# Attention and two MoE layers on one core: loads of sums moved ahead of raw weights, low parts on VectorE, norms and output copies on ScalarE

## The chip, the cores and the metric

One NeuronCore of a Trainium2 chip runs the whole computation. The metric is the device time of one execution in microseconds (us). Five engines with in-order queues take part: PE (TensorE, the matmuls; its weight loads are listed as PEld), DVE (VectorE), ACT (ScalarE), POOL (GpSimd) and SP (SyncE, which here only issues DMAs).

## The reference

Three steps follow one another; the output of each is the input of the next.

1. Attention over q, k, v of 4 batches, 8 heads, 576 tokens, 64 values. *Downsampled*: q, k, v are averaged over groups of 4 tokens to 144, a softmax attention runs on those, and its result is repeated 4 times. *Local*: a softmax attention over the keys with |i - j| < 4. The two results are added and laid out as x, 2304 tokens x 512.
2. MoE 1: `(silu(x @ w_gate) * (x @ w_val)) @ w_out`, inner width 1536.
3. MoE 2: `h = x @ w_in; (h * clip(h + 3, 0, 6) / 6) @ w_out`, inner width 2048.

## The kernel before

**Weights.** The weights arrive as raw 8-byte floats. The chip decodes each to fp32 once, in block 0: `decode_a` (L208, ScalarE, the top bits) and `decode_b` (L217, VectorE, the rest). The fp32 form is written to DRAM (`kept`) and loaded again in the later blocks. A *unit* is 128x512 weights. `split_unit` cuts it into a high part (L228, ScalarE, tile `wr`) and a low part, weight minus high part (L231, also `wr`). `POOL_SPLIT = {1: 4}` puts every fourth low part of block 1 on GpSimd (17 of 68); all others are VectorE's. `prefetch(i)` issues the steps of a unit ahead of its use: the raw load 8 units ahead, the load from `kept` 6, the decoding 5 and 4, the split 2.

**Blocks.** The tokens go through in five blocks of 512, 384, 512, 512 and 384 tokens (0 to 4). In each, 68 units follow one another in `run_unit`. Phase 1 (36 units) is MoE 1: G (`pG`), V (`pV`) and O (`aO`). Phase 2 (32 units) is MoE 2: H (`pH`) and P (`aP`). Each product is made of three matmul passes from high and low parts. Between the products VectorE and ScalarE work on the inner values: `sl` (L953, L959), `h` (L962, L963), `gV` and `gH` (L964, L965), and the high and low part of x in `put_cols` (L265, L266). At the end of a block `put_out` copies the four (or three) output banks, even ones by ScalarE (L1014), odd ones by VectorE (L1012), and SP sends them out.

**Attention inside the blocks.** x of the first batch is made in the front, before block 0 (`first_batch`: scores `fS`, row maxima `fnm`, exponentials `held`, values `fO`, sums `fxf`). The local attention of the other three batches is cut into chunks that run on VectorE beside the products of blocks 0 to 3: scores (L781, L784) in phase 1, values (L818 to L824, tile `o`) in phase 2; then PE turns `o` around (`px`, L838), `xf` adds the downsampled part (L847) and `put_cols` writes x of a later block. The downsampled attention of batch b+1 runs in block b, for b = 0, 1, 2:

- `down_sums`: twelve loads (`nq`, `nk`, `nv`, four each) and two GpSimd additions for each (L290, L291). For batch 1 they stand in the front, with six buffers; for batches 2 and 3 in phase 1 of blocks 1 and 2, with two buffers, driven once in two units.
- `down_main`, in phase 2: for each of four head pairs the scores (`pS`, L872), the maxima and exponentials (L697 on VectorE, L701 on ScalarE), then `norm_d` one unit later: L707 and L708 on VectorE make 1/sum (72x2), L709 on VectorE multiplies the 72x288 probabilities by it. Then PE transposes them (`pPT`, L715) and multiplies by the values (`pO`, L722).

**What sets the order.** The code issues instructions in the order above, and a scheduler makes one in-order queue for each engine. In the front, `behind` and `late` keep the steps of the weights and the loads in the order in which the code writes them. Buffers also order things: raw weights have four (`w64`), so the load of unit 4 waits on SP's queue for the decoding of unit 0.

Of the kernel before, what the change touches and what calls it, by code (L numbers as in the profile page):

```python
# [10 lines left out]
F32 = mybir.dt.float32  # L11
# [6 lines left out]
AF = mybir.ActivationFunctionType  # L18
# [15 lines left out]
CLOAD = (0, 4)  # L34

EARLY = 6

POOL_SPLIT = {1: 4}


@with_exitstack
def tile_kernel(
# [85 lines left out]
    def behind(ins):  # L128

        if front[0]:  # L130
            tc.keep_in_program_order(ins)
# [93 lines left out]
    def split_unit(i):  # L225
        s = view(w32[i // 2], i)
        r = sp.tile([P, 2, NC, P], F32R, tag="wr", name=f"wr{i}", bufs=4)
        behind(nc.scalar.activation(r[:, 0], s, AF.Copy))  # L228
        n = POOL_SPLIT.get(units[i][2])
        eng = nc.gpsimd if n and i % n == 0 else nc.vector  # L230
        behind(eng.tensor_tensor(r[:, 1], s, r[:, 0].bitcast(F32), op=ALU.subtract))  # L231
        split[i] = r

    def prefetch(i):
# [37 lines left out]
    def load_down(b, what, half, hh, alloc, eng):  # L272
        src = {"q": q, "k": k, "v": v}[what]
        t = alloc(f"n{what}{b}_{half}{hh}")
        late(
            eng, t,
            src[b, hh * 4:hh * 4 + 4, half * NJH * 4:(half + 1) * NJH * 4, :].rearrange("h (j t) d -> j h t d", t=4),
        )
        nat[b, what, half, hh] = t

    def down_sums(b, dn, qk, alloc, bufs, eng):
        keys = [(w, half, hh) for w in "qkv" for half in range(2) for hh in range(2)]
        for w in "qkv":
            dn[w] = sp.tile([NJH, 2, H, D], F32, tag="dn" + w, name=f"dn{w}{b}", bufs=1)
        for m in range(bufs):
            load_down(b, *keys[m], alloc, eng)
        for n, key in enumerate(keys):
            w, half, hh = key
            t = nat.pop((b, *key))
            nc.gpsimd.tensor_tensor(t[:, :, 0:2], t[:, :, 0:2], t[:, :, 2:4], op=ALU.add)  # L290
            nc.gpsimd.tensor_tensor(dn[w][:, half, hh * 4:hh * 4 + 4], t[:, :, 0], t[:, :, 1], op=ALU.add)  # L291
            if n + bufs < len(keys):
                load_down(b, *keys[n + bufs], alloc, eng)
            yield
# [23 lines left out]
    def first_batch():  # L318
# [6 lines left out]
        with tc.tile_pool(name="fp", bufs=1) as fp:  # L325
# [41 lines left out]
            def load_vd(n):  # L367
                hh, half = divmod(n, 2)
                t = fp.tile([NJH, H // 2, 4, D], F32, tag="vnat", name=f"vd4{half}{hh}", bufs=2)
                late(  # L370
                    nc.sync, t,
                    v[0, 4 * hh:4 * hh + 4, half * NJH * 4:(half + 1) * NJH * 4, :].rearrange(
                        "h (j t) d -> j h t d", t=4
                    ),
                )
                nc.gpsimd.tensor_tensor(t[:, :, 0:2], t[:, :, 0:2], t[:, :, 2:4], op=ALU.add)
                nc.gpsimd.tensor_tensor(vd[:, half, 4 * hh:4 * hh + 4], t[:, :, 0], t[:, :, 1], op=ALU.add)
# [20 lines left out]
            def values_of(i):  # L398
                return vw[i][:, i % 2].rearrange("p (h d) -> p h d", h=H)

            for n in range(2):
                load_vd(n)
                load_vw(n)
            prefetch(-LR)
            prefetch(1 - LR)
            for n in range(2, 4):
                load_vd(n)
                load_vw(n)
            load_vw(4)
            assert NT == 5  # L410
            prefetch(2 - LR)

            tmp = spare("tmp")
            at = 0
# [232 lines left out]
            for c in range(NC):  # L647
                load_T("q", c)
                load_T("k", c)
                if c:  # L650
                    down_scores(c - 1)
                sums(c)
                if c == 2:
                    prefetch(3 - LR)
                if c >= 2:
                    down_trans(c - 2)
            down_values(0)
            scores(0)
            down_scores(3)
            down_trans(2)  # L660
# [45 lines left out]
    def norm_d(pd, sd):  # L706
        nc.vector.tensor_scalar(sd, sd, EPS, 4.0, op0=ALU.add, op1=ALU.mult)  # L707
        nc.vector.reciprocal(sd, sd)  # L708
        nc.vector.tensor_tensor(pd, pd, sd[:, :, None].to_broadcast([NJH, 2, NJ]), op=ALU.mult)  # L709

    def trans_d(pd, ps):
        pt = ps[:NJH, :2 * NJ].rearrange("p (g j) -> p g j", g=2)
# [292 lines left out]
    def put_out(bi, e, ps):  # L1005
        if e == 0:

            done = sp.tile([P, NC, 2, UMAX * UT], F32R, tag="x2", name=f"os{bi}", bufs=1).bitcast(F32)
            state["os"] = done.rearrange("p c a t -> p (c a t)")
        os = state["os"][:, e * DM:(e + 1) * DM]  # L1010
        if e % 2:
            nc.vector.tensor_copy(os, ps)  # L1012
        else:
            nc.scalar.activation(os, ps, AF.Copy)  # L1014
        gu = starts[bi] + 2 * e
        (b, u), (b1, _) = divmod(gu, NG), divmod(gu + 1, NG)
        for n, m in ((0, 2),) if b == b1 else ((0, 1), (1, 1)):
            b, u = divmod(gu + n, NG)
            if b == 0:
                dst = out[(gu + n) * UT:(gu + n + m) * UT, :]  # L1020
            else:
                dst = flat(out, (b * S + u * 4) * DM, [[DM, 4 * m], [SL * DM, NSEG], [1, DM]])
            nc.sync.dma_start(dst, os[n * UT:(n + m) * UT, :])
# [115 lines left out]
```

## Time and profile before

| | us |
|---|---|
| median of 3 runs | 1001.62 (1001.51 to 1006.58) |
| the profiled execution | 1001.4 |
| its span | 999.3 |
| PE busy | 955.3 (96%) |
| DVE busy | 787.6 (79%) |
| ACT busy | 510.6 (51%) |
| POOL busy | 137.2 (14%) |

The profile is of one execution. Its own time is 2.1 us over its span (what lies around the span), and 0.2 us below the median. A busy share is a mean over stages that differ: in the front PE waits for attention, in phase 2 of block 1 VectorE has more to do than in blocks 3 and 4, and GpSimd has work in the front and in blocks 1 and 2 only. The mean granted TensorE clock of the span is 0.984 of full speed.

### The profile page before, as it was taken

The page shows a single profiled execution, that of the slowest core. Times are in us where ns is not written, and L with a number is a line of the kernel's source. Part 1 is how long each engine was busy: PE and PEld are TensorE (multiplying, and loading weights), DVE is VectorE, ACT ScalarE, POOL GpSimd, SP SyncE. Part 2 cuts the span into 40 slices and gives each one's busy share as a digit, 9 for nine tenths or more (in the row PEclk, how much of TensorE's full clock was granted, in tenths as well). Part 3 has the DMA queues.
Part 4 walks back from the last instruction along what each step waited for, and adds up shares of the span by engine and source line. Part 5 has one row for each costly group of instructions (what it writes and reads, how often), then busy time and mean ns, then how long its engine had stood idle before and what let it go on. Part 6 is the DMA issues. An engine that isn't in the chain of part 4 may idle for free.

```text
span 999.3 us, 13482 instructions
## 1 busy us (share of the span) xinstructions
PE 955.3 (96%) x4800; PEld 796.1 (80%) x4800; DVE 787.6 (79%) x1251; ACT 510.6 (51%) x1058; POOL 137.2 (14%) x130
## 2 busy tenths in 40 slices
PE   8769999999998999879999999999999999999997
PEld 5658888778797987767878777788888788999996
DVE  6698986899999879998985699999346995545653
ACT  4667566766543475444333654443335444544653
POOL 5680000000068211103630000000000000000000
PEclk9789999999999999999999999999999999999999
DMA  9979999377677532245753212354322233533331
GB/s 194 211 222 318 304 321 319 115 248 262 222 238 219 179 107 80 85 148 164 222 172 115 76 64 93 124 191 141 104 85 90 85 100 111 157 125 124 124 123 50
DMA packets 83655, 160.72 MB, mean 161 GB/s; under 512 B 19460, under 2 KB 51716, under 8 KB 83588
## 3 DMA queue, kind: packets, MB, share of 16 engines
q1 hardware_dynamic: 78692, 142.03, 45.4%
q10 hardware_dynamic: 4896, 17.83, 5.1%
q8 instruction: 38, 0.62, 0.3%
q14 instruction: 29, 0.24, 0.1%
HBM read 137.29 MB, written 22.54 MB: 160 GB/s over the span
## 4 chain that ended last, share of the span: by engine, by line
PE 78%; DVE 14%; ACT 2%; issue 2%; DMA 2%; SPq 0%; ACTq 0%; DVEq 0%
PE aP L989 19%; PE pH L947 19%; PE aO L989 13%; PE pG L947 12%; PE pV L947 11%; DVE wr L231 3%; DVE pr L781 2%; DVE sc L784 1%; PE pS L872 1%; DVE gV L965 1%; ACT held L561 1%; PE pO L722 1%; DMA w<-kept 1%; DVE sl L959 1%; DMA w<-in_moe_w_val_dram 1%
## 5 line engine op out<-in xcount | busy, mean ns | idle before, releaser
L231 DVE TENSOR_TENSOR wr<-w,wr 128x512 fp32r<-128x512 f32 x323 | 235.1, 731 | 106.3 <-ACT wr L228 104.7
L228 ACT ACTIVATE wr<-w 128x512 fp32r<-128x512 f32 x340 | 212.1, 626 | 170.5 <-PE aP L989 58.7
L947 PE MATMUL pH<-x,wr 128*128 128x512 f32 (+1 forms) x960 | 217.2, 376 | 4.2 <-DVE wr L231 4.2
L989 PE MATMUL aP<-wr,gH 128*128 128x512 f32 x864 | 216.9, 400 | 0.7 <-DVE wr L231 0.7
L947 PEld LDWEIGHTS pH<-x,wr 128*128 128x128 f32 x960 | 173.6, 188 | 33.0 <-DVE wr L231 5.5
L989 PEld LDWEIGHTS aP<-wr,gH 128*128 128x128 f32 x864 | 160.5, 189 | 38.4 <-issue 2.3
L947 PE MATMUL pG<-xr,wr 128*128 128x512 f32 (+3 forms) x732 | 158.9, 371 | 10.8 <-ACT xr L265 4.2
L989 PE MATMUL aO<-gV,wr 128*128 128x512 f32 (+1 forms) x720 | 157.8, 375 | 2.9 <-DVE wr L231 2.9
L947 PEld LDWEIGHTS pG<-xr,wr 128*128 128x128 f32 x732 | 133.9, 192 | 30.4 <-ACT xr L265 4.3
L947 PE MATMUL pV<-xr,wr 128*128 128x512 f32 (+1 forms) x720 | 153.1, 368 | 0.0
L989 PEld LDWEIGHTS aO<-gV,wr 128*128 128x128 f32 x720 | 132.8, 190 | 22.7 <-DVE wr L231 3.6
L947 PEld LDWEIGHTS pV<-xr,wr 128*128 128x128 f32 x720 | 131.0, 188 | 16.7
L962 ACT ACTIVATE h<-pH,half 128x512 f32<-128x512 f32 (+1 forms) x80 | 51.6, 645 | 75.8 <-PE pH L947 75.5
L963 DVE SCALAR_TENSOR_TENSOR h<-h,pH 128x512 f32<-128x512 f32 (+1 forms) x80 | 50.4, 631 | 25.1 <-ACT h L962 24.0
L953 ACT ACTIVATE sl<-pG 128x512 f32<-128x512 f32 (+1 forms) x60 | 33.2, 554 | 64.6 <-PE pG L947 64.3
L964 ACT ACTIVATE gV<-sl 128x512 fp32r<-128x512 f32 (+1 forms) x60 | 35.2, 587 | 57.5 <-DVE sl L959 56.8
L781 DVE TENSOR_TENSOR pr<-q,k 128x1792 f32<-128x1792 f32 x27 | 58.8, 2178 | 6.7 <-DMA k<-in_k_dram 6.7
L231 POOL TENSOR_TENSOR wr<-w,wr 128x512 fp32r<-128x512 f32 x17 | 23.2, 1363 | 288.6 <-DVE h L963 195.2
L208 ACT ACTIVATE top<-w 128x512 f16<-128x512 bf16 x68 | 53.0, 790 | 10.4 <-DMA w<-in_moe_w_in_dram 4.0
L964 ACT ACTIVATE gH<-h 128x512 fp32r<-128x512 f32 (+1 forms) x80 | 46.9, 587 | 19.3 <-DVE h L963 17.3
L965 DVE TENSOR_TENSOR gH<-h,gH 128x512 fp32r<-128x512 f32 (+1 forms) x80 | 51.9, 650 | 3.6 <-ACT gH L964 2.6
L818 DVE TENSOR_TENSOR pv<-sc,v 128x1792 f32<-128x1792 f32 x27 | 54.5, 2018 | 0.2
(128 smaller groups left out, 825.1 us busy)
## 6 DMA issues: line engine op xcount, KB each, us to landing
w<-kept SPq DMA_DIRECT2D x136, 512.0 KB
kept<-w ACTq DMA_DIRECT2D x34, 512.0 KB
w<-in_moe_w_out_dram SPq DMA_DIRECT2D x28, 512.0 KB
w<-in_moe_w_in_dram SPq DMA_DIRECT2D x16, 512.0 KB
w<-in_moe_w_gate_dram SPq DMA_DIRECT2D x12, 512.0 KB
w<-in_moe_w_val_dram SPq DMA_DIRECT2D x12, 512.0 KB
out_dram<-os SPq DMA_DIRECT2D x16, 256.0 KB
nq<-in_q_dram SPq DMA_DIRECT2D x12, 288.0 KB
```

The costliest lines, as they stand in the source:

```text
L208: behind(nc.scalar.activation(halves(top[i % 2], 2, F16)[:, :, 1], h3.bitcast(BF16), AF.Copy))
L228: behind(nc.scalar.activation(r[:, 0], s, AF.Copy))
L231: behind(eng.tensor_tensor(r[:, 1], s, r[:, 0].bitcast(F32), op=ALU.subtract))
L781: nc.vector.tensor_tensor(pr, qt[:, a:a + SUB, None, :].to_broadcast([P, SUB, W, D]), win(kt, a, SUB), op=ALU.mult)
L818: nc.vector.tensor_tensor(pr, pe[:, a:a + SUB, :, None].to_broadcast([P, SUB, W, D]), win(vt, a, SUB), op=ALU.mult)
L947: nc.tensor.matmul(ps[:, cs], r[:, a, c], x[:, c, b_, cs], start=part is HIGH and a == c == 0, stop=part is LOW and c == NC - 1,)
L953: nc.scalar.activation(sl, ps, AF.Silu)
L962: nc.scalar.activation(h, ps, AF.Relu, scale=1 / 6, bias=half1[:, 0:1])
L963: nc.vector.scalar_tensor_tensor(h, h, 1.0, ps, op0=ALU.min, op1=ALU.mult)
L964: nc.scalar.activation(g[:, 0, :nt], h, AF.Copy)
L965: nc.vector.tensor_tensor(g[:, 1, :nt], h, g[:, 0, :nt].bitcast(F32), op=ALU.subtract)
L989: nc.tensor.matmul(ps, **one, start=f_ == 0 and a == b_ == 0, stop=f_ == nf - 1 and b_ == 1,)
```

## The change

Four edits, independent of one another.

1. *Front.* The raw loads of the first four units (`prefetch(-8)` to `prefetch(-5)`) stood among the loads of `vd` and `vw` and at step c = 2. They now stand behind the first step of `down_sums`, which issues the six loads of `nq` and `nk`. `down_sums` gets a `yield` of its own after those loads, so in blocks 1 and 2, too, the first sum comes one step later than its loads.
2. *Low parts.* `POOL_SPLIT` goes; VectorE makes all 340 low parts.
3. *Norms.* The multiplication L709 (VectorE, one 72x288) becomes two ScalarE activations with a scale for each row (72x144 each).
4. *Output copies.* The odd banks are copied by ScalarE as well, but for the last block.

```diff
--- before.py
+++ after.py
@@ -34,8 +34,6 @@
 CLOAD = (0, 4)
 
 EARLY = 6
-
-POOL_SPLIT = {1: 4}
 
 
 @with_exitstack
@@ -226,9 +224,7 @@
         s = view(w32[i // 2], i)
         r = sp.tile([P, 2, NC, P], F32R, tag="wr", name=f"wr{i}", bufs=4)
         behind(nc.scalar.activation(r[:, 0], s, AF.Copy))
-        n = POOL_SPLIT.get(units[i][2])
-        eng = nc.gpsimd if n and i % n == 0 else nc.vector
-        behind(eng.tensor_tensor(r[:, 1], s, r[:, 0].bitcast(F32), op=ALU.subtract))
+        behind(nc.vector.tensor_tensor(r[:, 1], s, r[:, 0].bitcast(F32), op=ALU.subtract))
         split[i] = r
 
     def prefetch(i):
@@ -284,6 +280,7 @@
             dn[w] = sp.tile([NJH, 2, H, D], F32, tag="dn" + w, name=f"dn{w}{b}", bufs=1)
         for m in range(bufs):
             load_down(b, *keys[m], alloc, eng)
+        yield
         for n, key in enumerate(keys):
             w, half, hh = key
             t = nat.pop((b, *key))
@@ -398,17 +395,11 @@
             def values_of(i):
                 return vw[i][:, i % 2].rearrange("p (h d) -> p h d", h=H)
 
-            for n in range(2):
-                load_vd(n)
-                load_vw(n)
-            prefetch(-LR)
-            prefetch(1 - LR)
-            for n in range(2, 4):
+            for n in range(4):
                 load_vd(n)
                 load_vw(n)
             load_vw(4)
             assert NT == 5
-            prefetch(2 - LR)
 
             tmp = spare("tmp")
             at = 0
@@ -650,11 +641,12 @@
                 if c:
                     down_scores(c - 1)
                 sums(c)
-                if c == 2:
-                    prefetch(3 - LR)
                 if c >= 2:
                     down_trans(c - 2)
             down_values(0)
+            next(ahead)
+            for n in range(4):
+                prefetch(n - LR)
             scores(0)
             down_scores(3)
             down_trans(2)
@@ -706,7 +698,8 @@
     def norm_d(pd, sd):
         nc.vector.tensor_scalar(sd, sd, EPS, 4.0, op0=ALU.add, op1=ALU.mult)
         nc.vector.reciprocal(sd, sd)
-        nc.vector.tensor_tensor(pd, pd, sd[:, :, None].to_broadcast([NJH, 2, NJ]), op=ALU.mult)
+        for half in range(2):
+            nc.scalar.activation(pd[:, half], pd[:, half], AF.Copy, scale=sd[:, half:half + 1])
 
     def trans_d(pd, ps):
         pt = ps[:NJH, :2 * NJ].rearrange("p (g j) -> p g j", g=2)
@@ -1008,7 +1001,7 @@
             done = sp.tile([P, NC, 2, UMAX * UT], F32R, tag="x2", name=f"os{bi}", bufs=1).bitcast(F32)
             state["os"] = done.rearrange("p c a t -> p (c a t)")
         os = state["os"][:, e * DM:(e + 1) * DM]
-        if e % 2:
+        if e % 2 and bi == NB - 1:
             nc.vector.tensor_copy(os, ps)
         else:
             nc.scalar.activation(os, ps, AF.Copy)
```

SP's queue in the front, before (`vd`, `vw`: values of the first batch; `w_n`: raw weights of unit n):

```order
L124 DMA vd_241<-in_v_dram 72x4x256
L124 DMA vw_238<-in_v_dram 128x8x64
L188 DMA w_0_246<-in_moe_w_gate_dram 128x4x512
L188 DMA w_1_248<-in_moe_w_gate_dram 128x4x512
L124 DMA vd_250<-in_v_dram 72x4x256
L124 DMA vw_254<-in_v_dram 128x8x64
L124 DMA vd_256<-in_v_dram 72x4x256
L124 DMA vw_254<-in_v_dram 128x8x64
L124 DMA vw_261<-in_v_dram 3x8x64
L124 DMA vw_261<-in_v_dram 91x8x64
L188 DMA w_2_264<-in_moe_w_val_dram 128x4x512
L188 DMA w_3_397<-in_moe_w_val_dram 128x4x512
```

and after:

```order
L122 DMA vd_252<-in_v_dram 72x4x256
L122 DMA vw_250<-in_v_dram 128x8x64
L122 DMA vw_257<-in_v_dram 3x8x64
L122 DMA vw_257<-in_v_dram 91x8x64
L122 DMA nq_00_481<-in_q_dram 72x4x256
L122 DMA nq_01_483<-in_q_dram 72x4x256
L122 DMA nq_10_485<-in_q_dram 72x4x256
L122 DMA nq_11_487<-in_q_dram 72x4x256
L122 DMA nk_00_489<-in_k_dram 72x4x256
L122 DMA nk_01_491<-in_k_dram 72x4x256
L186 DMA w_0_493<-in_moe_w_gate_dram 128x4x512
L186 DMA w_1_495<-in_moe_w_gate_dram 128x4x512
```

The six loads of the sums have moved ahead of all raw weights, `w_0` and `w_1` by twelve places down the queue.

GpSimd's queue at the end of the front and the start of block 1, before (`w_68` is the first unit of block 1):

```order
L290 TENSOR_TENSOR nv_11_777<-nv_11_777 72x4x128
L291 TENSOR_TENSOR dnv_554<-nv_11_777 72x256
L231 TENSOR_TENSOR wr_2797<-w_68_2706,wr_2797 128x512
L290 TENSOR_TENSOR nq_00_2877<-nq_00_2877 72x4x128
L291 TENSOR_TENSOR dnq_2874<-nq_00_2877 72x256
L231 TENSOR_TENSOR wr_2887<-w_72_2795,wr_2887 128x512
L290 TENSOR_TENSOR nq_01_2879<-nq_01_2879 72x4x128
L291 TENSOR_TENSOR dnq_2874<-nq_01_2879 72x256
L290 TENSOR_TENSOR nq_10_2883<-nq_10_2883 72x4x128
L291 TENSOR_TENSOR dnq_2874<-nq_10_2883 72x256
L290 TENSOR_TENSOR nq_11_2929<-nq_11_2929 72x4x128
L231 TENSOR_TENSOR wr_2985<-w_76_2885,wr_2985 128x512
```

and after:

```order
L287 TENSOR_TENSOR nv_11_777<-nv_11_777 72x4x128
L288 TENSOR_TENSOR dnv_480<-nv_11_777 72x256
L287 TENSOR_TENSOR nq_00_2885<-nq_00_2885 72x4x128
L288 TENSOR_TENSOR dnq_2882<-nq_00_2885 72x256
L287 TENSOR_TENSOR nq_01_2887<-nq_01_2887 72x4x128
L288 TENSOR_TENSOR dnq_2882<-nq_01_2887 72x256
L287 TENSOR_TENSOR nq_10_2933<-nq_10_2933 72x4x128
L288 TENSOR_TENSOR dnq_2882<-nq_10_2933 72x256
```

The low parts between the sums are gone from this queue; the sums follow one another.

VectorE's queue at the first norms of phase 2 of block 1, before:

```order
L963 SCALAR_TENSOR_TENSOR h_1_3706<-h_1_3706,pH_1_3692 128x384
L707 TENSOR_SCALAR sd_0_3714<-sd_0_3714 72x2
L708 RECIPROCAL sd_0_3714<-sd_0_3714 72x2
L709 TENSOR_TENSOR pd_0_3713<-pd_0_3713,sd_0_3714 72x288
L707 TENSOR_SCALAR sd_1_3720<-sd_1_3720 72x2
L708 RECIPROCAL sd_1_3720<-sd_1_3720 72x2
L965 TENSOR_TENSOR gH_1_3705<-h_1_3706,gH_1_3705 128x384
L709 TENSOR_TENSOR pd_1_3719<-pd_1_3719,sd_1_3720 72x288
```

VectorE after:

```order
L227 TENSOR_TENSOR wr_3747<-w_108_3622,wr_3747 128x512
L956 SCALAR_TENSOR_TENSOR h_1_3714<-h_1_3714,pH_1_3700 128x384
L699 TENSOR_SCALAR sd_0_3722<-sd_0_3722 72x2
L700 RECIPROCAL sd_0_3722<-sd_0_3722 72x2
L699 TENSOR_SCALAR sd_1_3728<-sd_1_3728 72x2
L700 RECIPROCAL sd_1_3728<-sd_1_3728 72x2
L958 TENSOR_TENSOR gH_1_3713<-h_1_3714,gH_1_3713 128x384
L689 TENSOR_REDUCE nm_2_3769<-pS_2_3731 72x2
```

and ScalarE after:

```order
L693 ACTIVATE pd_0_3721,sd_0_3722<-pS_0_3691,nm_0_3719 72x144
L955 ACTIVATE h_1_3714<-pH_1_3700,half_101 128x384
L693 ACTIVATE pd_0_3721,sd_0_3722<-pS_0_3691,nm_0_3719 72x144
L693 ACTIVATE pd_1_3727,sd_1_3728<-pS_1_3692,nm_1_3725 72x144 x2
L957 ACTIVATE gH_1_3713<-h_1_3714 128x384
L702 ACTIVATE pd_0_3721<-pd_0_3721,sd_0_3722 72x144 x2
L702 ACTIVATE pd_1_3727<-pd_1_3727,sd_1_3728 72x144 x2
L955 ACTIVATE h_2_3764<-pH_2_3750,half_101 128x384
```

L709 has left VectorE; a low part (L227, unit 108) stands there that was GpSimd's. ScalarE has four activations more (L702) between `gH` of one unit and `h` of the next. In the changed kernel L231 is L227, L707 and L708 are L699 and L700, L709 is L702, L963 is L956, L965 is L958, L962 is L955, L964 is L957, L701 is L693.

## Rows read from the trace of the kernel before

**Rows 1.** The page's first part: busy time, share of the span, instructions
```profile
PE 955.3 (96%) x4800; PEld 796.1 (80%) x4800; DVE 787.6 (79%) x1251; ACT 510.6 (51%) x1058; POOL 137.2 (14%) x130
```

**Rows 2.** Stretches: length, busy of PE, PEld, DVE, ACT, POOL, clock, DMA, GB/s
```profile
0.00:72.15 72.15, 53.88 (x427) 38.24 (x427) 53.28 (x95) 41.60 (x159) 49.12 (x65) 0.86 0.86 204
72.15:273.94 201.79, 201.77 (x938) 160.65 (x939) 177.13 (x293) 133.46 (x249) 1.41 (x1) 0.99 0.78 264
273.94:358.98 85.04, 78.90 (x449) 77.67 (x448) 75.83 (x80) 36.13 (x69) 44.24 (x33) 0.98 0.65 207
358.98:451.73 92.75, 83.01 (x444) 67.58 (x443) 87.88 (x178) 49.31 (x122) 9.52 (x7) 0.98 0.29 98
523.33:999.30 475.97, 468.96 (x2253) 397.10 (x2251) 329.67 (x548) 223.74 (x417) 0.00 (x0) 1.00 0.34 109
849.65:995.70 146.05, 142.69 (x769) 136.01 (x767) 77.40 (x128) 71.43 (x129) 0.00 (x0) 1.00 0.37 118
```

**Rows 3.** Waits of PE in 273 to 452: total, times, longest
```profile
PE pH L947 <- DVE wr L231: 4.2, 3, 2.8
PE px L838 <- DVE o L824: 4.1, 3, 2.9
PE aO L989 <- DVE wr L231: 2.9, 1, 2.9
PE pG L947 <- POOL wr L231: 2.1, 1, 2.1
```

**Rows 4.** Groups by form: busy, mean ns, idle before them
```profile
L818 DVE TENSOR_TENSOR pv<-sc,v 128x1792 f32<-128x1792 f32 x27 | 54.5, 2018 | 0.2
...
L231 POOL TENSOR_TENSOR wr<-w,wr 128x512 fp32r<-128x512 f32 x17 | 23.2, 1363 | 288.6 <-DVE h L963 195.2 <-ACT wr L228 79.4 <-PE pPT L715 14.0
...
L701 ACT ACTIVATE pd<-pS,nm 72x144 f32<-72x144 f32 x48 | 17.5, 370 | 3.2 <-DVE nm L697 2.5 <-DVE sm L811 0.6
...
L709 DVE TENSOR_TENSOR pd<-pd,sd 72x288 f32<-72x288 f32 x24 | 10.7, 448 | 0.2
...
L1012 DVE COPY os<-aP 128x512 f32<-128x512 f32 x8 | 5.5, 686 | 6.6 <-PE aP L989 6.6
```

**Rows 5.** Timeline of DVE and POOL, 280 to 307: start, us, engine, line
```profile
280.03 1.92 DVE L231 TENSOR_TENSOR wr<-w,wr 128x512 fp32r<-128x512 f32 x1
280.12 1.28 POOL L231 TENSOR_TENSOR wr<-w,wr 128x512 fp32r<-128x512 f32 x1
...
306.19 0.68 DVE L231 TENSOR_TENSOR wr<-w,wr 128x512 fp32r<-128x512 f32 x1
306.79 0.54 DVE L959 TENSOR_TENSOR sl<-sl,pV 128x384 f32<-128x384 f32 x1
```

**Rows 6.** Timeline of DVE and POOL, 416 to 435
```profile
416.02 0.20 DVE L813 TENSOR_TENSOR sc<-sc,sm 128x56 f32<-128x56 f32 x1
...
434.25 1.29 POOL L231 TENSOR_TENSOR wr<-w,wr 128x512 fp32r<-128x512 f32 x1 [11.62 <-ACT wr L228]
...
434.29 1.31 DVE L813 TENSOR_TENSOR sc<-sc,sm 128x56 f32<-128x56 f32 x1
```

**Rows 7.** Timeline of DVE and POOL, 383 to 405
```profile
383.19 1.29 POOL L231 TENSOR_TENSOR wr<-w,wr 128x512 fp32r<-128x512 f32 x1 [7.88 <-ACT wr L228]
...
383.24 1.19 DVE L847 TENSOR_TENSOR xf<-px,odT 64x128 f32<-64x128 f32 x4
...
404.01 1.19 DVE L847 TENSOR_TENSOR xf<-px,odT 64x128 f32<-64x128 f32 x4
```

**Rows 8.** Timeline of SP, POOL, DVE and PE in the front
```profile
28.30 1.98 SPq L188 DMA_DIRECT2D w<-in_moe_w_val_dram  x1
...
37.95 1.26 POOL L290 TENSOR_TENSOR nq<-nq 72x512 f32<-72x512 f32 x1 [4.91 <-DMA nq<-in_q_dram]
...
39.39 1.17 DVE L217 SCALAR_TENSOR_TENSOR w<-w,top 128x512 int32<-128x512 int32 x1
...
57.74 0.38 PE L947 MATMUL pG<-xr,wr 128*128 128x244 f32 x1 [4.16 <-ACT xr L265]
```

## The prediction, made before the changed kernel ran

> **What bounds the kernel now.** I read the page's busy shares first, then a table of stretches, then the waits of TensorE in the worst stretch, then the timelines of VectorE and GpSimd at the places where the waits end. PE is busy 955.3 of 999.3 us, VectorE 787.6, ScalarE 510.6, GpSimd 137.2 [rows 1]. The stretches show where the other 44 us of PE lie [rows 2]: 18.3 in the front (0 to 72.15), nothing in block 0 (201.77 of 201.79), 6.1 in phase 1 of block 1 (85.04 against 78.90), 9.7 in its phase 2 (92.75 against 83.01), the rest thinly in the later blocks (7.0 from 523.33 on). Block 1 is the place that this change touches most: VectorE is busy 75.8 of 85.0 and then 87.9 of 92.8 us there, while ScalarE is busy 36.1 and 49.3. Block 4 has the same tokens and no attention, and its last stretch takes 146.05 us with VectorE at 77.4. PE's waits in block 1 end at VectorE's low parts (4.2 and 2.9 us), at VectorE's attention values (`px`, 4.1) and once at GpSimd's low part (2.1) [rows 3]. So block 1 is bound by VectorE in turns with PE. A 2% lower granted clock (0.98 against 1.00 in blocks 2 to 4) goes with those idle times.
>
> **Low parts (edit 2).** The 17 that leave GpSimd took 1.36 us each there [rows 4]. On VectorE a low part that nothing disturbs takes 0.68, and the next instruction begins 0.60 after it began (306.19 to 306.79) [rows 5]. So VectorE gets 17 x 0.60 = 10.2 us more. Against this stands what GpSimd's low parts cost VectorE now. At 280.03 a VectorE low part that runs beside GpSimd's (280.12, 1.28 us) takes 1.92 in place of 0.68, 1.24 too much [rows 5]. At 434.29 the 128x56 product beside the last of the 17 takes 1.31 in place of 0.20, 1.11 too much [rows 6]. I set each of the 17 beside the VectorE instruction that overlaps it in the same way; the first shown and the last are those two, the excess lies between 0 and 1.24, and it adds up to 13.8 us: 8.7 for the ten that belong to phase 1, 5.1 for the seven of phase 2. Net, VectorE gains 8.7 - 6.0 = 2.7 us in phase 1 and 5.1 - 4.2 = 0.9 in phase 2.
>
> An instruction that reads PSUM does not show this: the four 64x128 additions at 383.24 begin 0.05 us after GpSimd's low part and take 1.19, as the four at 404.01 do with GpSimd idle [rows 7]. The Trainium skill says the same of the two engines (SBUF — State Buffer, Who interferes with whom): a VectorE instruction with two SBUF inputs and a GpSimd instruction that reads SBUF exclude each other for a whole instruction. Rows 5 and 7 agree; by that rule the lost time ends when GpSimd's instruction is gone, and the sums L290 and L291, which stay, go on costing.
>
> **Norms (edit 3).** VectorE loses 24 instructions of 0.448 us [rows 4]; with the overlap of 0.08 seen above some 0.38 each on its queue, 9.1 in all, 3.0 in block 1 (8 of them). ScalarE gets 48 activations of 72x144. The trace has no copy of that shape with a scale; the exponentials of that shape take 0.370 busy [rows 4], so 48 x 0.37 = 17.8 us is the upper end, of which 5.9 in block 1, where ScalarE has 43 of 93 us free in phase 2. They stand in ScalarE's queue between `gH` of one unit and `h` of the next, and they wait for the reciprocals on VectorE. Behind them wait `h`, the high parts and so VectorE's low parts. In block 0 PE never waits, so that there the move costs and gains nothing.
>
> **Output copies (edit 4).** Seven of eight copies of 0.686 us [rows 4] leave VectorE. Two belong to the end of block 0 and fall at the start of phase 1 of block 1, one to the end of block 1; with overlap 0.6 each, 1.2 in phase 1 and 0.6 in phase 2. ScalarE does up to four in a row instead of two. No product waits for the output's way to DRAM. I take those 1.8 us of VectorE's time in block 1, and nothing elsewhere; the bounds are as much lost, should the weights' high parts wait behind the copies, and 3 x 0.69 = 2.1 gained.
>
> **Sum for block 1.** Phase 1: VectorE -2.7 - 1.2 = -3.9; PE's 2.1 us wait for GpSimd's low part falls into this. The granted clock gives back at most 2% of 85 = 1.7; I take 0.6 of it. -4.5, with bounds -8.5 (all 6.1 of idle, 1.7 of clock and 0.7 of stalls that do not show as PE's idle) and +3 (the low parts' 6.0 in full with only half of the stalls given back, since the sums now run without a break and meet VectorE elsewhere). Phase 2: -0.9 - 3.0 - 0.6 = -4.5, and 0.5 of the clock: -5, with bounds -12 (9.7 of idle, 1.9 of clock, rounded up) and +3 (ScalarE held at the norms of block 1: four pairs by 0.75).
>
> **Front (edit 1).** GpSimd waits 4.91 us for the first `nq` and begins at 37.95 [rows 8]; its load stands behind raw weights that are still being issued at 28.30. With these out of the way the sums begin up to 4 us earlier and end so much earlier. The decoding of units 0 and 1 on VectorE (1.17 us at 39.39, and one like it) moves behind the maxima of the fourth score tile. PE's first product at 57.74 waits 4.16 us for x, not for weights [rows 8]; the chain that makes x passes VectorE. So about 2 us of decoding no longer stand ahead of x, but the same 2 us then come in the stretch just before block 0, in place of one low part and one later decoding that fall behind the last x. Gain 0 to 4 from the earlier sums and x; loss 0 to 4 if the raw weights are late (unit 4's load waits for unit 0's decoding, which now comes later). I take -1.5. What is won or lost here passes to the end in full, since PE is full in block 0.
>
> **Other blocks.** In block 0 norms and copies have no wait of PE to end: 0. In block 2 the sums' loads come one step before the sums, so that GpSimd waits less, and eight norms leave VectorE: PE's idle there from 523.33 on is 7.0 us for all of blocks 2 to 4, mostly away from the norms. I take -0.5, with bounds -3 and +2.
>
> **The sum.** -1.5 - 4.5 - 5 - 0.5 = -11.5 us on the profiled execution's 1001.4: 989.9, and as the median of the runs lies 0.2 above that execution, 990. Its own range: half of the distance to each bound, all parts seldom on one side: 984 to 995.5.
>
> **Rivals.**
>
> A. *The low parts come home at their own price.* The stalls that go are stalls of instructions after which VectorE waited anyway, or the sums take over: then 17 x 0.60 = 10.2 eats what comes back, and only norms (3.0) and copies (0.6 of the 1.2) in block 1 count, with no more than 0.5 in the front: 1001.4 - 4.1 = 997.3. For it: VectorE is idle 9.2 of 85 us in phase 1, and the sums still collide. Against it: 87.9 of 92.8 us busy in phase 2 leaves little waiting. The Trainium skill (Perfetto Trace Analysis, Optimizing Scalar/DVE Operations) says that work of a saturated VectorE may go to ScalarE or even GpSimd, which speaks for the norms' move and against bringing low parts back; it adds that moving work between VectorE and GpSimd might not help, as they share a port. Rows 5 are a case of its second half. By its first half alone edit 2 would cost those 10.2 us.
>
> B. *Slower: ScalarE is held at the norms.* It runs its queue in order, and each pair of norms waits for reciprocals that on VectorE stand behind products of 2.02 us (L818) [rows 4]. While it waits, `h`, `gH` and the next high part wait, then the low part, then PE. There are twelve head pairs. With the rest of the forecast at -11.5, it is slower than before from 11.5/12, about 1 us of PE's time for each pair; at 1.5 us each (a 2.02 us product less half a microsecond of slack) it is +18, so 1001.4 + 6.5 = 1008. For it: the reciprocals are ready late in phase 2, where VectorE is 95% busy. Against it: the norms are issued one unit after their exponentials, and units there take about 2.9 us (92.75/32).
>
> C. *All of block 1's idle time goes.* VectorE's queue was the only reason for it; then 6.1 + 9.7 us and the clock's 3.6 come back: 1001.4 - 19.4 - 1.5 = 980.5. Against it: VectorE stays over 85% busy there, and 24 sums go on disturbing it in phase 1.
>
> **How the numbers follow.** Forecast 0.62, A 0.18, B 0.11, C 0.09. A difference of 0.5%, 5 us, is about what a measurement of this kernel can tell from no change: faster is below 996.6, slower above 1006.6. The forecast's range and C lie on the faster side, with a little of A: 0.72. A makes most of no change: 0.17. B makes slower: 0.11. The range for 8 in 10 takes in the forecast, almost to C's end on one side and through A on the other: 981 to 999.
>
> **What would show it.** Edit 2: VectorE's low parts in block 1 near 0.7 us apart from the sums', no 1.9 in phase 2, and PE's waits for low parts in block 1 under half of 9.2. Edit 3: ScalarE's 72x144 copies at 0.25 to 0.37 us, with little idle time before them that ends at the reciprocals; a microsecond or more there, and `h` late behind it, is B. Edit 1: block 0's first full run of products begins 0 to 4 us before 72.15, and the first `nq` sum before 37.95; a PE wait for the first low part instead says the raw weights are late. Block 1's two stretches should take about 80.5 and 87.8 us. If phase 1 stays at 85 with VectorE as busy as before, it is A. The forecast is wrong in its mechanism if block 1 keeps its idle time while the total falls, or if the end moves by more than the front and block 1 together.

## The result, and the profile after

The changed kernel takes 1015.54 us (median of 4, 1014.0 to 1016.38) against 1003.28 on the same chip: a ratio of 1.0118, with a 95% interval of 1.0096 to 1.0141. It is 12 us slower, where 11.5 less were forecast, and outside of the range. The profiled execution has a span of 1014.5 us. The first part of its page, which answers to [rows 1]:

```profile
PE 966.8 (95%) x4797; PEld 804.6 (79%) x4800; DVE 778.9 (77%) x1237; ACT 528.4 (52%) x1113; POOL 113.2 (11%) x113
```

VectorE and GpSimd did lose work, and ScalarE gained it. But PE, whose work is the same, is busy 11.5 us longer, and it is idle 3.7 us longer (47.7 against 44.0). Together that is 15.2 us, more than the 12 of the medians: the execution profiled of the kernel before is one of its shortest (1001.4). Where the time goes, the table of stretches tells. Cut at the last product of each phase or block, the kernel before has (phases 1 and 2 of block 1, block 2; columns as in [rows 2]):

```profile
274.10:359.10 85.00, 78.86 (x450) 77.63 (x449) 75.79 (x80) 36.09 (x69) 44.24 (x33) 0.98 0.65 207
359.10:453.50 94.40, 84.66 (x451) 68.92 (x450) 88.93 (x180) 50.42 (x124) 9.52 (x7) 0.98 0.30 101
453.50:660.00 206.50, 203.62 (x945) 160.43 (x944) 177.64 (x272) 94.09 (x192) 32.92 (x24) 1.00 0.42 131
```

and the changed kernel:

```profile
276.90:361.10 84.20, 80.17 (x450) 78.22 (x449) 73.37 (x86) 36.62 (x70) 34.80 (x24) 0.98 0.70 210
361.10:457.40 96.30, 87.55 (x451) 72.73 (x451) 87.16 (x179) 55.16 (x141) 0.00 (x0) 0.93 0.30 99
457.40:672.90 215.50, 207.04 (x944) 162.31 (x943) 174.87 (x261) 100.12 (x210) 32.90 (x24) 0.98 0.40 125
```

Block 2 is 9.0 us longer, block 1 1.1 us in sum, 2.8 us are lost before 276.90, and some 2.7 in blocks 3 and 4. PE's idle time is a stretch's length less its busy time. In block 2 it rises from 2.9 to 8.5 us. In phase 2 of block 1 it falls from 9.7 to 8.8, while PE's busy time rises by 2.9 at a lower granted clock, 0.93 against 0.98: there it isn't waiting that makes the phase longer. The waits of PE over the whole span name the place in block 2 (of the rows, the first and those that answer to [rows 3]):

```profile
PE pqT L300 <- POOL dnq L288: 8.3, 2, 6.1
...
PE pH L940 <- DVE wr L227: 3.7, 1, 3.7
PE aO L982 <- DVE wr L227: 2.7, 4, 1.8
PE px L831 <- DVE o L817: 2.6, 2, 2.3
```

GpSimd's low part is gone from the list, as forecast. New at its head is a wait for GpSimd's sums. The timeline of PE there:

```profile
468.02 2.97 PE L940 MATMUL pG<-xr,wr 128*128 128x512 f32 x12
473.26 0.28 PE L300 MATMUL pqT<-ident,dnq 72*128 72x72 f32 x1 [2.28 <-POOL dnq L288]
479.61 0.62 PE L300 MATMUL pqT<-ident,dnq 72*128 72x72 f32 x3 [6.07 <-POOL dnq L288]
479.98 4.97 PE L940 MATMUL pG<-xr,wr 128*128 128x512 f32 x12
```

and of GpSimd:

```profile
470.82 2.39 POOL L288 TENSOR_TENSOR dnq<-nq 72x256 f32<-72x256 f32 x1
473.17 1.71 POOL L287 TENSOR_TENSOR nq<-nq 72x512 f32<-72x512 f32 x1
...
478.51 1.05 POOL L288 TENSOR_TENSOR dnq<-nq 72x256 f32<-72x256 f32 x1
484.07 1.29 POOL L287 TENSOR_TENSOR nq<-nq 72x512 f32<-72x512 f32 x1 [4.51 <-DMA nq<-in_q_dram]
```

The first four transposes of GpSimd's sums (`pqT`) of block 2 stand 21 units earlier in PE's queue than before: at place 868, behind block 2's fifth unit (before: at place 920, behind its 26th, where they began at 528.8). The first waits for the first q sum. The second needs the third sum, which ends at 479.56, and the other two stand behind it. PE's queue is in order, so all products wait behind them. PE does one transpose in the 8.6 us from 471.0 on, and the granted clock falls to its lower level, 0.50, from 474.0 to 484.2, so the first products after the wait run slower as well (12 in 4.97 us):

```profile
474.00:484.20 10.20, 4.59 (x13) 3.72 (x14) 8.29 (x7) 1.56 (x3) 4.38 (x5) 0.50 0.90 280
```

The places in PE's queue around the first transposes, of the changed kernel:

```
867 L940 MATMUL pG_2_4695<-xr_3844,wr_4640 128x512 x12
868 L300 MATMUL pqT_0_5218<-ident,dnq_4631 128x72 x4
869 L940 MATMUL pG_3_4717<-xr_3844,wr_4660 128x512 x12
```

There is a second loss, spread thinly. Two units of V in block 3, which nothing disturbs, and two of O, in the kernel before:

```profile
665.30 5.60 PE L947 MATMUL pV<-xr,wr 128*128 128x512 f32 x24
...
681.62 5.75 PE L989 MATMUL aO<-gV,wr 128*128 128x512 f32 x24
```

and two of V in the changed kernel:

```profile
678.40 5.76 PE L940 MATMUL pV<-xr,wr 128*128 128x512 f32 x24
```

That is 240 ns for each 512-column matmul in place of 233, as a group's length over its 24 (from start to start it is 233 in place of 227, as the last one's length counts in full in the group's). The clock is no reason: block 3 as a stretch has PE full and a granted clock of 1.00 in the kernel before,

```profile
660.00:849.80 189.80, 189.80 (x829) 154.22 (x829) 137.30 (x207) 83.54 (x141) 0.00 (x0) 1.00 0.34 110
```

and in the changed kernel, where it is 1.9 us longer:

```profile
672.90:864.60 191.70, 191.70 (x830) 154.28 (x829) 136.28 (x206) 84.78 (x143) 0.00 (x0) 1.00 0.33 109
```

The slower pace holds for G and V (the products that read x) in every block; O, H and P took 240 already. With 864 such matmuls of 512 columns at 6.7 ns and 576 of 384 columns at 2.2 (182 against 180 ns) it comes to 7 us, an estimate; the experiments below give 4 to 5.

### The profile page after: what moved, and what is told of

It reads as the page before. It is cut to its first block, busy times and chain, and to the rows that moved or that the text cites. A ratio compares the mean times of both kernels' runs of the same rounds, so it can differ in the third digit from the quotient of the medians.

```text
span 1014.5 us, 13514 instructions
## 1 busy us (share of the span) xinstructions
PE 966.8 (95%) x4797; PEld 804.6 (79%) x4800; DVE 778.9 (77%) x1237; ACT 528.4 (52%) x1113; POOL 113.2 (11%) x113
## 4 chain that ended last, share of the span: by engine, by line
PE 73%; issue 14%; DVE 7%; DMA 2%; ACT 2%; POOL 1%; SPq 0%; ACTq 0%; DVEq 0%; POOLq 0%
PE pH L940 16%; PE aP L982 16%; PE aO L982 12%; PE pG L940 12%; PE pV L940 12%; DVE wr L227 1%; DMA nv<-in_v_dram 1%; ACT held L552 1%; DVE w L215 1%; DVE pr L774 1%; PE pS L865 1%; DVE sc L777 1%; PE pO L715 1%; PE warm L90 1%; DMA k<-in_k_dram 1%
## 5 line engine op out<-in xcount | busy, mean ns | idle before, releaser
L227 DVE TENSOR_TENSOR wr<-w,wr 128x512 fp32r<-128x512 f32 x340 | 241.9, 715 | 116.3 <-ACT wr L226 114.8
L940 PE MATMUL pH<-x,wr 128*128 128x512 f32 (+1 forms) x960 | 219.5, 379 | 3.7 <-DVE wr L227 3.7
L940 PEld LDWEIGHTS pH<-x,wr 128*128 128x128 f32 x960 | 176.2, 191 | 31.8 <-DVE wr L227 4.4
L940 PE MATMUL pG<-xr,wr 128*128 128x512 f32 (+3 forms) x732 | 162.5, 378 | 4.3 <-ACT xr L261 4.3
L940 PE MATMUL pV<-xr,wr 128*128 128x512 f32 (+1 forms) x720 | 157.0, 373 | 1.3 <-DVE wr L227 1.3
L940 PEld LDWEIGHTS pG<-xr,wr 128*128 128x128 f32 x732 | 136.9, 195 | 24.4 <-ACT xr L261 4.6
L955 ACT ACTIVATE h<-pH,half 128x512 f32<-128x512 f32 (+1 forms) x80 | 51.5, 644 | 72.8 <-PE pH L940 72.5
L956 DVE SCALAR_TENSOR_TENSOR h<-h,pH 128x512 f32<-128x512 f32 (+1 forms) x80 | 50.4, 631 | 26.1 <-ACT h L955 25.4
L774 DVE TENSOR_TENSOR pr<-q,k 128x1792 f32<-128x1792 f32 x27 | 58.9, 2181 | 6.1 <-DMA k<-in_k_dram 6.0
L287 POOL TENSOR_TENSOR nq<-nq 72x512 f32<-72x512 f32 x12 | 18.2, 1516 | 351.9 <-DMA nq<-in_q_dram 351.9
L957 ACT ACTIVATE gH<-h 128x512 fp32r<-128x512 f32 (+1 forms) x80 | 46.9, 588 | 17.4 <-DVE h L956 15.1
L215 DVE SCALAR_TENSOR_TENSOR w<-w,top 128x512 int32<-128x512 int32 x68 | 49.7, 733 | 6.9 <-ACT top L206 6.4
L777 DVE TENSOR_REDUCE sc<-pr 128x28 f32<-128x1792 f32 x27 | 54.3, 2010 | 0.1
```

Source lines behind the costliest of these rows:

```text
L215: behind(nc.vector.scalar_tensor_tensor(w32[i // 2][:, i % 2].bitcast(I32), h12, 13, top[i % 2], op0=ALU.logical_shift_right, op1=ALU.bitw ...
L227: behind(nc.vector.tensor_tensor(r[:, 1], s, r[:, 0].bitcast(F32), op=ALU.subtract))
L774: nc.vector.tensor_tensor(pr, qt[:, a:a + SUB, None, :].to_broadcast([P, SUB, W, D]), win(kt, a, SUB), op=ALU.mult)
L777: nc.vector.tensor_reduce(sc[:, a:a + SUB], pr, axis=AX.X, op=ALU.add)
L940: nc.tensor.matmul(ps[:, cs], r[:, a, c], x[:, c, b_, cs], start=part is HIGH and a == c == 0, stop=part is LOW and c == NC - 1,)
L955: nc.scalar.activation(h, ps, AF.Relu, scale=1 / 6, bias=half1[:, 0:1])
```

## The experiments

Ratios are to the kernel before on the same chip, with 95% intervals. "At 160" and "at 32" are places in on-chip memory, explained under Place.

| run | edits | median us | ratio |
|---|---|---|---|
| e1 | all, transposes pinned | 1009.14 | 1.0055 (1.003 to 1.008) |
| e2 | all, no late step | 1014.92 | 1.0122 (1.0097 to 1.0147) |
| e3 | low parts | 999.50 | 0.9973 (0.9956 to 0.9989) |
| e4 | norms | 1006.71 | 1.0038 (1.0015 to 1.006) |
| e5 | front, without the later step in blocks 1 and 2 | 1008.19 | 1.0037 (1.0021 to 1.0052) |
| e6 | e5, x at its old place | 1003.56 | 0.9998 (0.9979 to 1.0017) |
| e7 | none, x at 32 | 1008.57 | 1.0051 (1.0033 to 1.0069) |
| e8 | none, the products' operands all at 160 | 995.68 | 0.9917 (0.9891 to 0.9944) |
| e9 | low parts, all at 160 as in e8 | 991.50 | 0.9887 (0.9868 to 0.9907) |
| e10 | norms but block 1's | 1003.56 | 0.9997 (0.998 to 1.0013) |
| e11 | all, pinned, x at its old place | 1002.64 | 0.9994 (0.9979 to 1.001) |
| e12 | low parts and norms | 1004.02 | 1.0011 (0.9994 to 1.0028) |
| e13 | none, the products' operands all at 32 | 995.96 | 0.9927 (0.9902 to 0.9952) |
| e14 | norms of block 1 | 1009.34 | 1.0061 (1.0039 to 1.0084) |
| e15 | copies | 1005.86 | 1.0032 (1.0015 to 1.0048) |

**Order (e1, e2, e12).** e1 keeps the transposes behind what the code writes ahead of them:

```diff
-                        nc.tensor.transpose(
+                        one = nc.tensor.transpose(
...
+                        if not front[0]:
+                            tc.keep_in_program_order(one)
```

> The changed kernel, with the transposes of the sums (pqT, pkT) kept behind everything that the code writes ahead of them on PE. Theory 1 (order): the changed kernel loses because the first pqT of block 2 stands right behind its fifth unit in PE's queue and waits 8.3 us for GpSimd's sums, with a lower granted clock after it; with the transposes at their old place that wait is gone and the time falls by 8 to 13 us against the changed kernel, to 1000 to 1006. Theory 2 (the sums' loads come a step later): the sums stay late, PE waits for them at another transposition, and the time stays above 1011.

The time fell by 0.63% of the time before, some 6 us, to 1009, less than theory 1's 8 to 13. Block 2, again between last products:

```profile
455.50:664.30 208.80, 206.14 (x944) 162.00 (x943) 172.13 (x261) 100.09 (x210) 33.02 (x24) 0.99 0.41 129
```

It is 6.7 us shorter than in the changed kernel. Theory 2 fell with e2, which takes out the `yield` in blocks 1 and 2 (`if b == 1: yield`):

> The changed kernel without the extra step between the sums' loads and the first sum in blocks 1 and 2 (kept in the front). PE's queue still has the first pqT of block 2 behind its fifth unit. Theory 1 (order): PE still waits 5 to 9 us for GpSimd's q sums there, and the time stays at 1010 to 1016. Theory 2 (late step): the sums come two units earlier, the wait goes, 1000 to 1006.

No change of time, and PE still waits:

```profile
PE pqT L305 <- POOL dnq L293: 7.9, 2, 5.4
```

e12 joins edits 2 and 3 alone.

> Edits 2 and 3 together on the kernel before, x at its old place, no edit 1. Each alone left the first transposition of block 2 late in PE's queue (places 930 and 940); together they bring it to place 874, near the changed kernel's 868. Theory 1 (order): PE waits 4 to 9 us for GpSimd's q sums there, so that the time is 1006 to 1011, 4 to 6 us above the sum of the two edits (1004). Rival: the effects add up, 1002 to 1005, no wait.

Here the times add up, as the rival said. Only one of the four transposes had moved ahead, the one that needs the first sum, and it waited little:

```profile
468.47 0.30 PE L303 MATMUL pqT<-ident,dnq 72*128 72x72 f32 x1 [2.71 <-POOL dnq L291]
```

So in the changed kernel it is the other three, held until the third sum, that cost. What makes the scheduler move them is not shown.

**Place (e5, e6, e7, e8, e13).** In the built program the two buffers of x (`xr`) lie at bytes 76960 and 93344 of each partition before, at 60448 and 76832 after. Divided by 256, the old places leave 160 and the new ones 32 (160 and 32 modulo 256). Buffers get their place at their first use; edit 1 puts x's first use ahead of the raw weights'. The split weights (`wr`) lie at 160 in both, the inner values and MoE 2's input at 32.

> The kernel before with edit 1 alone, and only in the front (blocks 1 and 2 keep the sums' old step). Seen so far: in the changed kernel, and in both runs with edit 1, the 512-column matmuls of G and V take 240 ns each at their fastest, in the kernel before and the runs without edit 1 233; O, H and P take the same in all. Theory 4 (place): edit 1 makes the buffers of x in on-chip memory get their place before those of the raw weights, which moves x from byte 76960 to 60448 of each partition, and PE reads it slower there: G and V 240 ns here too, 7 us in all, so 0.5 to 1% slower than before. Rival (loads): the raw weights' later loads cost 1 to 4 us in the front and nothing after it; G and V at 233.

The two units of V in block 3 for e5, then e6:

```profile
670.12 5.76 PE L944 MATMUL pV<-xr,wr 128*128 128x512 f32 x24
```

e6 gives the raw weights' buffers their place before x's, and the loads then use them:

```diff
-            raw[i] = sp.tile([P, 4 * DM + 4], I16, tag="w64", name=f"w64_{i}", bufs=4)
+            if i not in raw:
+                raw[i] = sp.tile([P, 4 * DM + 4], I16, tag="w64", name=f"w64_{i}", bufs=4)
...
+            for n in range(4 if wide else 0):
+                raw[n] = sp.tile([P, 4 * DM + 4], I16, tag="w64", name=f"w64_{n}", bufs=4)
             tmp = spare("tmp")
```

> The kernel of the run before this one, with the raw weights' buffers given their place ahead of x's, so that x lies where it lay in the kernel before; the loads' order is that of edit 1. Theory 4 (place): G and V at 233 ns, 5 to 8 us less than with edit 1 alone, and what is left against the kernel before is edit 1's own effect on the front (-4 to +4 us). Rival: no difference from edit 1 alone.

```profile
671.51 5.60 PE L947 MATMUL pV<-xr,wr 128*128 128x512 f32 x24
```

All engines' queues are the same in e5 and e6. The loss of e5 is gone with the place, and the loads' order by itself is worth nothing within 2 us (0.9998, 0.9979 to 1.0017). e7 moves x from 160 to 32 in the kernel before, by writing `tmp = spare("tmp")` ahead of the first loads (`tmp` lies in x's first buffer). Other tiles move along, but keep their places modulo 256; no instruction differs.

> The kernel before with x's buffers alone given another place (ahead of the inner values and the raw weights, byte 44064 and 60448); no instruction changes. Theory 4 (place): G and V at 240 ns, 5 to 8 us slower than before. Rival: 233, no difference.

```profile
673.67 5.73 PE L947 MATMUL pV<-xr,wr 128*128 128x512 f32 x24
```

So the place alone costs 5 us (0.33% to 0.69%). e8 allocates the four raw buffers first of all, which brings the inner values and MoE 2's input to 160 as well:

> The kernel before with the raw weights' buffers given the first place, so that the inner values and the second layer's input lie 16512 bytes further on; x and the split weights stay. If the pace depends on the place of what PE reads, modulo 256 bytes (x was at 160, all else that PE streams at 32 but for the weights), O and H should go from 240 to about 233 ns too and P may, and the time fall by 4 to 12 us below before. If it does not, O, H and P stay at 237 to 240 and the time at 1001 to 1005.

Now O runs at 233 ns too, and so do H and P (in block 3, 24 matmuls of P take 5.76 us in the kernel before, 5.60 here and in e13; 14 of H take 3.43 and 3.33). The kernel gains 0.83% without a single instruction changed:

```profile
663.57 5.60 PE L950 MATMUL pV<-xr,wr 128*128 128x512 f32 x24
...
679.89 5.60 PE L992 MATMUL aO<-gV,wr 128*128 128x512 f32 x24
```

e13 brings all, the split weights too, to 32 (x, then the split weights, get their places ahead of the raw weights):

> The kernel before with x, the second layer's input, the inner values and the split weights all placed at 32 modulo 256 bytes of the partition. So far PE was fast (233 ns for 512 columns) where both its operands lay at 160, and slow (240) where one lay at 160 and the other at 32. If what counts is that both lie alike, all five kinds of products are at 233 here and the time is 4 to 12 us below before (992 to 1000), as with all at 160. If 32 itself is the slow place, all are at 240 and the time is 4 to 8 us above (1007 to 1012).

```profile
666.67 5.60 PE L949 MATMUL pV<-xr,wr 128*128 128x512 f32 x24
...
682.99 5.60 PE L991 MATMUL aO<-gV,wr 128*128 128x512 f32 x24
```

No place is slow by itself: PE takes 240 ns where its two operands lie 128 bytes apart modulo 256, and 233 where they lie alike. Only these two distances were tried.

**Low parts (e3, e9).** e3 sets `POOL_SPLIT = {}` in the kernel before.

> The kernel before with edit 2 alone: all low parts by VectorE. My prediction's account: block 1 shorter by 3 to 4 us, total 0.3 to 0.5% faster. Rival A (they come home at their price): within 0.1%. Theory 3 (low parts on VectorE are what makes the changed kernel slower): block 1 longer by 5 to 10 us, total 0.5 to 1% slower. PE's order has no early pqT here, so theory 1 expects no wait of PE for the sums in block 2.

A gain of 2.7 us, 0.27% (0.11% to 0.44%). Phases 1 and 2 of block 1:

```profile
275.30:356.20 80.90, 78.27 (x449) 76.12 (x449) 74.73 (x89) 36.24 (x69) 32.09 (x24) 1.00 0.71 219
356.20:454.30 98.10, 88.63 (x451) 72.78 (x450) 88.30 (x187) 51.04 (x124) 0.00 (x0) 0.93 0.30 97
```

Phase 1 is 4.1 us shorter and PE's idle time there falls from 6.1 to 2.6; for edit 2 the prediction had 2.7, and 0.6 of the clock. Some of this is the luck of one pair of executions: phase 1 takes 80.9 to 85.1 us in the seven profiled kernels with edit 2, 82.2 to 89.4 in the ten without. In phase 2 VectorE is busy 0.6 us less, where the forecast was 0.9, and its low parts take 0.68 each. Yet the phase is 3.7 longer in this execution, the longest of its ten. It isn't PE's idle time that grew there (9.5 against 9.7) but its busy time, by 4.0, at a granted clock of 0.93. On top of e8, e9 has the same gain in the medians, with intervals that overlap, and this is the fastest version:

> Edit 2 (all low parts by VectorE) on the kernel with the raw weights' buffers at the first place. If the two gains (0.27% and 0.83% against the kernel before) have nothing to do with each other, they add up: 0.7 to 1.5% faster than before, 988 to 997. If the low parts' gain was only PE's waiting moved about, it stays at the second one's 995 to 997.

**Norms (e4, e10, e14).** e4 has edit 3 alone; e10 and e14 split it with `act=b != 2` and `act=b == 2`, where `act` chooses ScalarE.

> The kernel before with edit 3 alone: norms on ScalarE. My prediction's account: block 1 shorter by 3 us, total 0.3% faster. Rival B (ScalarE's queue held at the norms): h and the high parts late, 5 us or more slower. PE's order has no early pqT here either, so theory 1 expects no wait of PE for the sums in block 2.

> Edit 3 alone, but with block 1's eight norms left on VectorE. Edit 3 alone cost 0.38%; its profile has phase 2 of block 1 at 98.8 us with a granted clock of 0.93 (before: 94.5 and 0.98), and no idle time of ScalarE before the norms in the changed kernel. Theory 5 (the cost lies in phase 2 of block 1: PE's rhythm there and with it the clock): without block 1's norms no loss, 1000 to 1004. Rival (cost spread over blocks 0 and 2, whose norms stay on ScalarE): 0.2 to 0.4% slower as before, 1005 to 1008.

> Edit 3 for the eight norms of block 1 alone. Theory 5 (edit 3 costs in block 1, 0.38% in all; without block 1's norms the ratio was 0.9997): 0.2 to 0.6% slower than before, 1005 to 1009. Rival (the cost came from the order in which the scheduler put other things, or from both parts together): within 0.15%.

The cost comes with block 1's eight norms alone. It isn't rival B. In the changed kernel ScalarE is not idle ahead of a norm:

```profile
L702 ACT ACTIVATE pd<-pd,sd 72x144 f32<-72x144 f32 x48 | 16.4, 412 | 0.0
```

PE's queue has changed here, too. At the end of block 1 PE waits for the last attention values (`o`) in the kernel before, turns them (`px`), and finishes P:

```profile
447.86 0.66 PE L838 MATMUL px<-ident,o 128*128 128x128 f32 x2 [2.95 <-DVE o L824]
448.37 3.52 PE L989 MATMUL aP<-wr,gH 128*128 128x512 f32 x9
...
451.96 1.55 PE L989 MATMUL aP<-wr,gH 128*128 128x512 f32 x6
```

e14:

```profile
449.61 0.63 PE L842 MATMUL px<-ident,o 128*128 128x128 f32 x2
449.89 2.79 PE L993 MATMUL aP<-wr,gH 128*128 128x512 f32 x7
...
453.60 3.65 PE L993 MATMUL aP<-wr,gH 128*128 128x512 f32 x15
```

After the last `px` 22 matmuls of P are left in e14 (24 in the changed kernel), 15 in the kernel before and in e10. That looks like a cost, but PE's idle time in phase 2 doesn't bear it out. It is 9.8 us in e14 against 9.7; what grows is PE's busy time, by 2.8 us, at a granted clock of 0.96 against 0.98:

```profile
359.90:457.20 97.30, 87.46 (x452) 71.00 (x451) 88.56 (x172) 54.86 (x140) 10.45 (x7) 0.96 0.29 98
```

Another 3.5 us of this execution lie in block 2 (210.0 us, 5.4 of them idle, against 206.5 and 2.9). So that block 1's norms cost is shown; why they do stays open.

**Copies (e15).** Edit 4 alone.

> Edit 4 alone: output copies on ScalarE. My prediction took 1.8 us of VectorE's time from block 1, 0.2% faster. If the parts add up (place +4.8, order +6, low parts -2.7, norms +3.8 against +11.9 in all), copies are within 0.2% of before. A cost of 0.3% or more would mean that ScalarE's high parts wait behind the copies.

It costs 0.32%. ScalarE at the end of block 0, before:

```profile
272.76 0.60 ACT L1014 ACTIVATE os<-aP 128x512 f32<-128x512 f32 x1 [2.19 <-PE aP L989]
273.51 1.27 ACT L228 ACTIVATE wr<-w 128x512 fp32r<-128x512 f32 x2
```

and in e15:

```profile
274.03 0.60 ACT L1014 ACTIVATE os<-aP 128x512 f32<-128x512 f32 x1 [0.80 <-PE aP L989]
274.77 0.63 ACT L228 ACTIVATE wr<-w 128x512 fp32r<-128x512 f32 x1
275.42 0.60 ACT L1014 ACTIVATE os<-aP 128x512 f32<-128x512 f32 x1
275.92 0.62 ACT L228 ACTIVATE wr<-w 128x512 fp32r<-128x512 f32 x1
```

Two high parts of block 1 now end at 276.5 in place of 274.8, between and behind copies that follow PE's pace. But this execution as a whole runs 1.3 us later here (its copies at 274.03 and 272.76), so that the second high part is 0.5 us late, and PE loses nothing by it. Its first product of block 1 and the one 14 us later keep the same 1.3, before:

```profile
273.94 4.35 PE L947 MATMUL pG<-xr,wr 128*128 128x384 f32 x24
...
287.95 4.32 PE L947 MATMUL pV<-xr,wr 128*128 128x384 f32 x24
```

and in e15:

```profile
275.22 4.35 PE L947 MATMUL pG<-xr,wr 128*128 128x384 f32 x24
...
289.24 4.32 PE L947 MATMUL pV<-xr,wr 128*128 128x384 f32 x24
```

Phase 1 of block 1 is 3.1 us longer in this execution, further on; single executions of kernels without edits 2 and 4 differ there by up to 7 us. Why the copies cost is not shown.

**Together (e11).** All four edits with both accidents mended:

> The changed kernel with x's buffers at their old place and the transposes of the sums at their old place in PE's queue; all four edits stay. If place and order are what made the changed kernel slower, the time is 8 to 13 us below it: 1001 to 1006, within 0.4% of the kernel before. My prediction's gain of 11.5 would need 990. If something else costs as well, it stays above 1008.

Place and order account for the whole loss: without them the change is worth nothing, 0.9994. Phases 1 and 2 of block 1 show what became of the gain, in one execution, the longest of ten:

```profile
277.10:360.50 83.40, 78.92 (x449) 76.00 (x449) 74.74 (x87) 36.24 (x70) 32.47 (x24) 1.00 0.69 212
360.50:458.10 97.60, 89.05 (x452) 74.04 (x451) 87.31 (x179) 55.10 (x141) 0.00 (x0) 0.91 0.29 98
```

Against the kernel before, PE's idle time falls by 1.7 and 1.2 us. But in phase 2 PE is busy 4.4 us longer, at a granted clock of 0.91 in place of 0.98. The ten executions of e11 have a mean granted clock of 0.975 over the span, and so have those of e12; the 25 of the kernel before on the same chip have 0.980. Of 1003 us that is 5 us of PE's full speed, an estimate and an upper one, as PE isn't busy all the time. With edit 2 or edit 3 alone (e3, e4) it is 0.979 and 0.978. What lowers the clock with both stays open.

## Why the prediction was wrong

- **Other blocks, -0.5 (bounds -3 and +2).** This term failed most. The prediction took the scheduler's order of PE as given and looked at the queues of the other engines. PE's queue carried the loss: transposes moved ahead of their sums, 6 us (e1). It also misread where PE was idle: 6.9 of the 7.0 us from 523.33 on lie behind PE's last product (992.4), and 2.8 between 451.73 and 523.33, which it has no row for; there the transposes came to stand.
- **Front, -1.5 (bounds -4 to +4).** The order of the loads is worth 0 (e6). The edit's cost came from what the prediction had no term for, the place of x, 4 us by e5 against e6 and 5 by e7. It isn't spent in the front: it is 6.7 ns in each G and V matmul of all blocks. The forecast's first step came true: the first `nq` sum begins at 30.43 in place of 37.95. The second didn't: x is no earlier for it, as PE's first product begins at 59.85 in place of 57.74 and waits 4.32 us for x.
- **Low parts.** Right in sign and near in size: 2.7 us less in all (e3), where 3.6 of VectorE's time and some clock were forecast. In the changed kernel phase 1 takes 84.2 us, not 80.5, and PE's waits for low parts in block 1 come to 7.7 us (3.7, 2.7 and 1.3), not to under half of 9.2. Rival A, by which edit 2 gains nothing, is outside of e3's interval.
- **Phase 2 of block 1, -5 (bounds -12 and +3).** Failed. It took VectorE's time as PE's time, and the clock as a gain. VectorE's work did fall as forecast: the durations of the phase's own instructions sum to 4.4 us less. A product of the next block (L774, 2.0 us) now falls into the phase, and VectorE's busy time, in which overlaps count once, fell by 1.8 (88.93 to 87.16). PE's idle time fell by 1.0 only, and the phase became 1.9 longer, with a granted clock of 0.93 in place of 0.98. The norms' share had the wrong sign (e14), and not for rival B's reason; on ScalarE each half takes 0.41 us, over the 0.37 that was called the upper end.
- **Copies, -1.8 (bounds +1.8 and -2.1).** The wrong sign: +3.2 (e15, interval 1.5 to 4.8), over the bound in the median. The bound's mechanism, high parts behind copies, is 0.5 us in the trace and doesn't reach PE.
- **Slower at all.** The rival with this sign, B, gave 1008 for a hold of ScalarE that is not in the trace.
- **The forecast's own range.** It is said to be half of the distance to each bound. Half of these distances, summed (16 below, 23.5 above), would be 982 to 1001.7, so 984 to 995.5 is narrower than its own rule; the result lies outside of both.
- The single edits do not quite add up: low parts -2.7, norms +3.8, copies +3.2, front 0 make +4.3, and e11 has -0.6 (interval -2.1 to +1.0). Each single one is uncertain by about 1.6 us or more; whether the copies cost less beside the other edits stays open.

## What to carry to other kernels

Where a scheduler makes the queues, an edit's largest effect may be an instruction that moves on an engine which the edit doesn't touch; compare the bounding engine's queue first, and pin what must not run ahead of a slow producer. Time freed on a helper engine counts only as far as the bounding engine's idle time falls by it. Set that engine's idle and busy time apart in each stretch: here a lower granted clock made the busy time longer by more than the waits gave back (e11). And compare the durations of undisturbed matmuls between two traces before explaining waits: a uniform shift there is no matter of scheduling.

## What the runs showed of the hardware

The place of PE's operands in on-chip memory matters, which I had not expected: 512-column matmuls take 233 ns each where the operand that PE streams and the one that it holds lie alike modulo 256 bytes, 240 where they lie 128 apart (e7, e8, e13; no other distance was run). Lining up all operands gave 0.7 to 0.8% with the instructions unchanged, and with the low parts on VectorE 1.1% (991.5 us).
